# Two turned rows sent from ACT's queue at an output burst, bursts of 6, 6 and 4 column blocks, and some roundings given to ACT

## The chip, the core and the metric

The kernel runs on one core of a Trainium2 chip. The core has five engines that work side by side, each through its own list of instructions in order: TensorE (PE in the profile; its weight loads are PEld), VectorE (DVE), ScalarE (ACT), GpSimd (POOL) and SyncE (SP). A transfer between the main memory and the core's buffers is issued by one of these lists too, and an instruction that waits holds all that stand behind it in its list. The metric is the time of one execution in microseconds (us), as the median of several runs.

## The reference

Two independent results are put side by side: a multi-query attention with 32 heads that share one key and one value head, and a discrete Fourier transform over both axes of a second input.

```python
# A: x (2048 x 1024), 32 heads of 32, one head for k and v
q = (x @ wq).reshape(B, S, H, Dh).transpose(0, 2, 1, 3)
k = x @ wk
v = x @ wv
p = softmax(einsum("bhqd,bkd->bhqk", q, k) * Dh ** -0.5)
a = einsum("bhqk,bkd->bhqd", p, v).transpose(0, 2, 1, 3).reshape(B, S, H * Dh) @ wo
# B: x (2048 x 1024), DFT matrices as inputs
re = einsum("bsd,ed->bse", x, dft_hid_re)
im = einsum("bsd,ed->bse", x, dft_hid_im)
b = einsum("ts,bse->bte", dft_seq_re, re) - einsum("ts,bse->bte", dft_seq_im, im)
return concatenate([a, b], axis=-1)      # all float32
```

## The kernel before

**Two kinds of work on TensorE.** The attention's scores and exponents are one kind. All other products (q, k, v, both stages of the DFT, the product with `wo`) are the other: they are called *fill products* and are put between the attention's matmuls, so that TensorE has work while the exponents are made.

**Fill products.** Each float32 operand is split into a rounded part (`hi`) and the difference that is left (`lo`), and a product of two blocks is three matmuls (hi·hi, hi·lo, lo·hi). A `Group` is one result of 128 x 512 with its left and right blocks. A block (`Item`) goes through four stages, which class `Line` counts in `n[0]` to `n[3]`: 0 `load` (from SP's queue), 1 `comb` (a sum or difference with a second source, on POOL), 2 `hi` (the rounding, function `cast`: on ACT in the start-up, on POOL later) and 3 `lo` (the difference, on POOL). `RL` is the line of the right blocks (tiles `r0`, `r1` as loaded, `rh`, `rl` as split), `ML` that of the left ones (`m0`, `m1`, `mh`, `ml`). The lines keep a few buffers each: `may` says whether a stage of the next block may be written yet, and `pump` writes a stage when the block's due time, counted in fill products (`pos["fill"]`), is near: 40 products ahead for the loads of right blocks and 14 for their rounding, 52 and 27 for left ones. Results go back to the main memory through `store`, nine products later, on SP's queue.

**The attention** runs in 32 units (4 query blocks of 512 x 8 groups of four heads), each of 32 steps. The loop `for n in range(total)` (line 753) writes one step: `score_step(n + 44)` makes row scores for a later unit (two matmuls into `pss`, the row maximum on DVE, and, one step later, the row exponents with their sum on ACT). `expo(n)` makes the exponents that are used: two matmuls into `pst` with the scores turned round (keys along partitions), and an exponent on ACT into a tile `p`. `pst` has one buffer and `pss` two. `level(n)` then writes some fill products, about five, so that they are spread evenly.

**The turned rows.** For each query of the unit the exponent needs two rows, the maximum and the logarithm of the sum, along the other axis. `lse_1`, `lse_1b` and `lse_2` work them out from the row maxima and sums, `lse_3` turns them on TensorE (a matmul with `ident`) and lets DVE copy the result into `mt`, and `lse_4` moves two rows of it into rows 96 and 97 of the unit's query tile `qst`, and a third (the inverse sums) to the main memory, `r_d`. A unit's first `expo` needs the two rows. In `score_step` the table `LSE` gives the step of the scores' count `e` (12 ahead of the exponents' count `r`) at which each of these is written; `TURN` is that of `lse_3`.

**The output burst.** `pv(u, k)` multiplies finished exponents with `v`. `CUT` says which of the 16 column blocks of `p` belong to each of the three bursts of a unit, and `ENDS`, twice that, at which steps they are written. A burst has four matmuls of the program per column block (eight records in the trace), all in one accumulator from `bank`, in which fill groups, bursts and `lse_3` take turns. In a step with a burst no fill products are written.

Of the kernel before, what the change touches and what calls it, by code (L numbers as in the profile page):

```python
# [16 lines left out]
P = 128  # L17
# [7 lines left out]
NC = 16  # L25
# [62 lines left out]
def tile_kernel(ctx: ExitStack, tc, xT, wq, wkv, wo, xbT, wT, cT, out):  # L88
    nc = tc.nc
    te = Ordered(tc, nc.tensor)  # L90
    act = Ordered(tc, nc.scalar)
    dve = Ordered(tc, nc.vector)
    gp = Ordered(tc, nc.gpsimd)
    sp = Ordered(tc, nc.sync)
# [11 lines left out]
    r_d = [dram.tile([NC, P], F32, name=f"r_{u}") for u in range(NQ * NG)]  # L106
# [26 lines left out]
    def move(q, to, of):  # L133
        q.dma_start(to.bitcast(F32), of.bitcast(F32))


    class Line:
# [24 lines left out]
        def pump(self):  # L162
            for k in range(4):
                while self.may(k) and self.items[self.n[k]].due - self.lead[k] <= pos["fill"]:
                    self.step(k)
# [3 lines left out]
                k = next(k for k in (3, 2, 1, 0) if self.may(k))  # L169
                self.step(k)  # L170

    pos = {"fill": 0, "s": 0}

    def cast(to, of):
        if pos["fill"] < START:
            act.activation(to, of, AF.Copy)
        else:
            gp.tensor_copy(to, of)
# [19 lines left out]
            sp.dma_start(it.t[-1], a)  # L198

    def comb(it):  # L200
        if it.pre:
            return
        for t, (_, sg) in zip(it.t[1:], it.srcs[1:]):
            (gp.tensor_add if sg > 0 else gp.tensor_sub)(it.t[0], it.t[0], t)
        if it.raw is not None:
            store(it.raw[0], it.t[0], it.raw[1])
# [39 lines left out]
    RL = Line(NR0, NR, (40, 40, 14, 8), load_r, comb, hi_r, lo)  # L246
    ML = Line(NM0, NM, (52, 36, 27, 21), load_m, comb, hi_m, lo)
# [28 lines left out]

    prev = {"set": -200, "this": 0}
    end = [0]

    def pump():  # L280
        RL.pump()
# [8 lines left out]
    def at(p, f):  # L290
        k = len(later)
        while k and later[k - 1][0] > p:
            k -= 1
        later.insert(k, (p, f))

    def run_later():
        while later and later[0][0] <= pos["fill"]:
            later.pop(0)[1]()
# [8 lines left out]
    def store(to, of, key=None):  # L307
        def go():
            move(sp, to, of)
            if key:  # L310
                ready.add(key)
        soon(go)
# [4 lines left out]
    def bank(name, open_=False):  # L317

        b = 1 - cur["bank"] if cur["bank"] is not None else int(used[1] < used[0])
        cur["at"] += 1  # L320
        used[b] = cur["at"]
        if open_:
            cur["bank"] = b
        return ps_b[b].tile([P, W], F32, name=name)
# [10 lines left out]
    def product(g, ps, j):  # L335
        c, w = divmod(j, 3)
        l, r = g.left[c // 4], g.right[c]
        a = (l.lo if w == 2 else l.hi)[:, c % 4]
        te.matmul(ps[:g.rows], a, r.lo if w == 1 else r.hi, start=j == 0, stop=j == g.n - 1)

    def take(n):
        for _ in range(n):
            if cur["group"] >= len(groups):
                return
            g = groups[cur["group"]]
            j = pos["fill"] - g.at
            if j == 0:
                cur["ps"] = bank("psb", True)
            if j % 3 == 0:
                RL.force(g.right[j // 3])  # L350
            if j % 12 == 0:
                ML.force(g.left[j // 12])
            product(g, cur["ps"], j)
            pos["fill"] += 1
            if j == g.n - 1:
                cur["group"] += 1
                assert all(hasattr(it, "done") for it in g.ys)
                g.post(cur["ps"])
                cur["at"] += 1
                used[cur["bank"]] = cur["at"]  # L360
                cur["bank"] = None
                if g.ys:
                    at(pos["fill"] + 2 * BEHIND, lambda n=len(g.ys): yused.__setitem__(0, yused[0] + n))
            pump()
            run_later()

    def aside():

        if cur["group"] >= len(groups):
            return  # L370
        g = groups[cur["group"]]
        j = pos["fill"] - g.at
        if 0 < j < 6:
            take(6 - j)
        elif j > g.n - 6:
            take(g.n - j)
# [180 lines left out]
    START = 24 * len(start)  # L557
# [13 lines left out]
    units = [(b, g) for b in range(NQ) for g in range(NG)]  # L571
    SU = 32
    LEAD = 12
    total = SU * len(units)
    qst, nm, lse, pt, ov, rb, pend = ({} for _ in range(7))
    ends = []

    def open_unit(u):
        b, g = units[u]
        assert ("q", b, g) in ready  # L580
        if u < 3:
            rows.append(qsp.tile([P, 4, W], F32R, name=f"qst{u}"))
            gp.memset(rows[u][96:P].bitcast(F32), 0.0)
        q = rows[u % 3]
        if u >= 3:
            move(sp, q[96:98].rearrange("p a b -> p (a b)"), kst[98:100])
        for r, src in enumerate((qh_d, ql_d, qh_d)):
            move(sp, q[r * DH:(r + 1) * DH], src[b][g].rearrange("(h d) c -> d h c", d=DH))
        qst[u] = q
        nm[u] = sm.tile([P, 10, NC], F32, name="nm")  # L590
# [43 lines left out]
    def lse_3(u):  # L634
        aside()
        pm = bank("psb")
        te.transpose(pm[:3 * NC, :P], nm[u][:, 3:6].rearrange("p a b -> p (a b)"), ident)
        mt = sm.tile([3 * NC, P], F32, name="mt")
        dve.tensor_copy(mt, pm[:3 * NC, :P])
        cur["at"] += 1  # L640
        lse[u] = mt

    def lse_4(u):
        mt = lse.pop(u)
        for a in range(2):
            move(sp, qst[u][96 + a:97 + a].rearrange("o h (t c) -> o (h t) c", c=P), mt[a * NC:(a + 1) * NC])
        sp.dma_start(r_d[u], mt[2 * NC:])

    def inverse(u):
        rb[u] = onp.tile([P, W], F32, name="rb")  # L650
# [10 lines left out]
            te.matmul(ps[:, a], kst[:, c * P:(c + 1) * P], qst[u][:, 2 * hp_ + a], start=True, stop=True)  # L661
        act.activation(pt[u, c, hp_], ps, AF.Exp)

    CUT = (0, 6, 11, NC)

    def pv(u, k):

        aside()
        ps = bank("psb")
        for c in range(CUT[k], CUT[k + 1]):  # L670
            for h in range(4):
                te.matmul(ps[h * DH:(h + 1) * DH], v[:, c], pt[u, c, h // 2][:, h % 2], start=c == CUT[k], stop=c == CUT[k + 1] - 1)
        if k == 0:
            ov[u] = onp.tile([P, W], F32, name="ov")
            dve.tensor_copy(ov[u], ps)
        else:
            dve.tensor_add(ov[u], ov[u], ps)
        cur["at"] += 1
        if k == len(CUT) - 2:
            b, g = units[u]  # L680
            hi_ = onp.tile([P, W], F32R, name="oh")
            lo_ = onp.tile([P, W], F32R, name="ol")
            lse["out"] = hi_, lo_

            last = u + 1 == len(units)
            e = dve if last else gp

            def low():
                e.tensor_sub(lo_, ov[u], hi_.bitcast(F32))
                if not last:  # L690
                    store(oh_d[b][g], hi_)
                    store(ol_d[b][g], lo_, ("o", b, g))

            ends.append(lambda: e.tensor_mul(ov[u], ov[u], rb[u]))
            ends.append(lambda: e.tensor_copy(hi_, ov[u]))
            ends.append(low)

    def score_step(s):

        if s < total:  # L700
            u, r = divmod(s, SU)
            if r == SU - 6 and u + 1 < len(units):
                open_unit(u + 1)
        if SU <= s < SU * (len(units) + 1) and s % SU == TURN:
            lse_3((s - SU) // SU)
        if s < total:
            scores(s)
        row_sums(s - 1)
        u, e = divmod(s - SU, SU)
        if 0 <= u < len(units):  # L710
            for f in LSE.get(e, ()):
                f(u)

    TURN = 6
    LSE = {1: (lse_1,), 2: (lse_1b,), 4: (lse_2,), 8: (lse_4,)}

    room = [(lambda t=t, k=k: t[:, k]) for t in [pp.tile([P, 2, W], F32, name="p") for _ in range(NP)] for k in range(2)]
    for n, (it, to) in enumerate(zip(RL.items, room)):
# [7 lines left out]
    take(66)  # L726
    for s in range(SU + LEAD):
        score_step(s)
        take(7)

    PRO = pos["fill"]
# [7 lines left out]
    def goal(n):  # L739
        return PRO + (FILL - PRO - LAST - MORE * (total - QUIET)) * n // total + MORE * max(n - QUIET, 0)  # L740


    ENDS = [2 * c for c in CUT]

    def level(n):
        r = n % SU
        if r in ENDS:
            return
        more = min(e for e in ENDS if e > r) - r
        left = goal(n + more) - pos["fill"]  # L750
        take(left - left * (more - 1) // more)

    for n in range(total):
        u, r = divmod(n, SU)
        if n == total - 12:
            w1 = wo_set(1)
            add([o_group(NQ - 1, t, e, ws) for e, ws in ((0, w0), (1, w1)) for t in range(4)])
        score_step(n + SU + LEAD)
        if ends:
            ends.pop(0)()  # L760
        expo(n)
        if r == 16:
            inverse(u)
        if r in ENDS and n:
            pv((n - 1) // SU, (ENDS.index(r) - 1) % (len(CUT) - 1))
        level(n)


    last = groups[len(groups) - 8:]
    take(last[0].at - pos["fill"] - 12)  # L770
    pv(len(units) - 1, len(CUT) - 2)
    while ends:
# [66 lines left out]
```

## Time and profile before

| | |
|---|---|
| median of 3 runs | 2813.01 us (2805.11 to 2813.58) |
| the profiled execution | 2811.13 us, span 2809.3 us |
| mean granted clock of TensorE | 0.996 |
| busy: TensorE, ACT, DVE, POOL | 2767.0, 2176.8, 1601.6, 1598.2 us |
| transfers | 489.73 MB, 174 GB/s in the mean |

All instructions carry line 66, that of the helper `Ordered` that records them, so groups are told apart by their tiles: `psb<-rh,mh` is a fill product, `pss<-kst,qst` row scores, `pst<-qst,kst` the turned scores, `psb<-p,v` a burst. In the table of waits a row names who waited, for whom, the total in us, how often and the longest. In the order of time a row has the start, the length, the engine and the instruction, and in brackets how long the engine idled before it and for whom. In a table of stretches a row has the stretch, its length, busy time and number of instructions of each engine, the granted clock, the share of the transfer engines and GB/s. SPq is SP's queue; a row there is the issue of a transfer, not its landing. The chain's rows have a start, a length and what the chain spent it on; a transfer there lasts from issue to landing.

### The profile page before, as it was taken

The numbers are of one execution on the slowest core, as the hardware profiler recorded it, in microseconds if no ns is written. First come the engines' busy times: TensorE is split into PE (matmuls) and PEld (weight loads), VectorE is DVE, ScalarE is ACT, GpSimd is POOL, SyncE is SP. The second block draws the span as 40 slices with busy tenths as digits, with TensorE's granted clock in tenths as the row PEclk, the third lists the DMA queues.
The fourth block names the chain that finished last, engine by engine and source line by source line (L and its number), as shares of the span: only waits on it lengthen the run. The fifth ranks groups of instructions, "written<-read, shape, count | busy, mean of one in ns | idle before, by whom it ended". The sixth has DMA issues, their size and how long they took to land.

```text
span 2809.3 us, 40359 instructions
## 1 busy us (share of the span) xinstructions
PE 2767.0 (98%) x13904; PEld 1936.5 (69%) x13904; DVE 1601.6 (57%) x1832; ACT 2176.8 (77%) x3151; POOL 1598.2 (57%) x1593
## 2 busy tenths in 40 slices
PE   8999999999999999999999999999999999999999
PEld 5876676676766766767666676667666667767666
DVE  6766666666666665555555555555555556556401
ACT  4578787888878888888878888878888778888740
POOL 3754524565536447766675575797787775540110
PEclk9999999999999999999999999999999999999999
DMA  7643325675676555665554464665565553554455
GB/s 257 196 147 113 125 87 188 218 240 181 214 241 207 165 161 186 185 184 149 167 193 133 150 188 140 195 211 173 186 201 169 177 185 105 169 175 150 123 168 170
DMA packets 320449, 489.73 MB, mean 174 GB/s; under 512 B 33978, under 2 KB 99002, under 8 KB 320186
## 3 DMA queue, kind: packets, MB, share of 16 engines
q1 hardware_dynamic: 320244, 487.15, 55.2%
q8 instruction: 110, 1.80, 0.3%
q14 instruction: 95, 0.78, 0.1%
HBM read 366.22 MB, written 119.28 MB: 173 GB/s over the span
## 4 chain that ended last, share of the span: by engine, by line
PE 89%; DMA 5%; POOL 2%; issue 2%; SPq 1%; ACT 1%; DVE 1%; POOLq 0%; ACTq 0%; DVEq 0%
PE psb L66 56%; PE pss L66 17%; PE pst L66 16%; DMA r<-s 2%; SPq L66 1%; POOL ml L66 1%; DMA qst<-mt 1%; POOL mh L66 0%; DMA p<-in_xT_dram 0%; ACT pss L66 0%; DMA m<-in_cT_dram 0%; POOL rh L66 0%; DMA r<-in_xT_dram 0%; ACT p L66 0%; DMA ql<-ql 0%
## 5 line engine op out<-in xcount | busy, mean ns | idle before, releaser
L66 DVE TENSOR_REDUCE nm<-pss 128x1 f32<-128x1024 f32 x1024 | 1252.6, 1223 | 594.6 <-PE pss L66 594.0
L66 ACT ACTIVATE p<-pst 128x1024 f32<-128x1024 f32 x1024 | 1053.4, 1029 | 487.2 <-PE pst L66 485.6
L66 ACT ACTIVATE pss<-pss,nm 128x1024 f32<-128x1024 f32 x1024 | 1112.9, 1087 | 69.0 <-DVE nm L66 66.7
L66 PE MATMUL psb<-rh,mh 128*128 128x512 f32 (+1 forms) x1852 | 730.9, 395 | 14.0 <-ACT rh L66 8.1
L66 PE MATMUL psb<-rh,ml 128*128 128x512 f32 (+1 forms) x1852 | 730.8, 395 | 6.4 <-POOL ml L66 6.4
L66 PE MATMUL psb<-rl,mh 128*128 128x512 f32 (+1 forms) x1852 | 729.2, 394 | 0.3 <-DVE rl L66 0.3
L66 PE MATMUL pst<-qst,kst 128*128 128x512 f32 x2048 | 654.4, 400 | 11.8 <-DMA qst<-mt 11.2
L66 PE MATMUL pss<-kst,qst 128*128 128x512 f32 x2048 | 654.8, 400 | 2.0 <-ACT pss L66 1.6
L66 PEld LDWEIGHTS pss<-kst,qst 128*128 128x128 f32 x2048 | 375.2, 188 | 162.8 <-issue 76.5
L66 POOL TENSOR_TENSOR ml<-m,mh 128x512 fp32r<-128x512 f32 x340 | 439.6, 1293 | 49.9 <-ACT mh L66 40.1
L66 PEld LDWEIGHTS pst<-qst,kst 128*128 128x128 f32 x2048 | 374.7, 188 | 128.8 <-ACT p L66 32.7
L66 PE MATMUL psb<-p,v 128*32 128x512 f32 x4096 | 462.5, 598 | 0.0
L66 PEld LDWEIGHTS psb<-rh,mh 128*128 128x128 f32 (+1 forms) x1852 | 346.9, 187 | 101.7 <-ACT rh L66 9.4
L66 PEld LDWEIGHTS psb<-rh,ml 128*128 128x128 f32 (+1 forms) x1852 | 346.8, 187 | 91.7 <-POOL ml L66 8.5
L66 PEld LDWEIGHTS psb<-rl,mh 128*128 128x128 f32 (+1 forms) x1852 | 346.8, 187 | 84.4 <-DVE rl L66 1.4
L66 POOL TENSOR_TENSOR r<-r,r 128x512 f32<-128x512 f32 x120 | 154.7, 1290 | 315.3 <-DMA r<-s 172.1
L66 PEld LDWEIGHTS psb<-p,v 128*32 128x32 f32 x4096 | 123.7, 110 | 286.9 <-issue 279.4
L66 POOL CAST mh<-m 128x512 fp32r<-128x512 f32 x339 | 208.3, 615 | 172.3 <-PE psb L66 155.9
L66 POOL CAST rh<-r 128x512 fp32r<-128x512 f32 x214 | 131.9, 616 | 264.2 <-PE psb L66 139.4
L66 POOL TENSOR_TENSOR rl<-r,rh 128x512 fp32r<-128x512 f32 x214 | 276.6, 1293 | 3.9
L66 POOL TENSOR_TENSOR m<-m,m 128x512 f32<-128x512 f32 x200 | 258.5, 1293 | 31.7 <-DMA m<-in_xbT_dram 19.6
L66 ACT ACTIVATION_READ_ACCUMULATOR pss<-pss,nm 128x1 f32 x1024 | 210.5, 206 | 0.0
(62 smaller groups left out, 690.5 us busy)
## 6 DMA issues: line engine op xcount, KB each, us to landing
m<-in_cT_dram SPq DMA_DIRECT2D x384, 256.0 KB
r<-s SPq DMA_DIRECT2D x192, 256.0 KB
y<-y SPq DMA_DIRECT2D x128, 256.0 KB
r<-in_wT_dram SPq DMA_DIRECT2D x88, 256.0 KB
m<-in_xbT_dram SPq DMA_DIRECT2D x88, 256.0 KB
y<-u SPq DMA_DIRECT2D x80, 256.0 KB
m<-in_wq_dram SPq DMA_DIRECT2D x64, 256.0 KB
qst<-qh SPq DMA_DIRECT2D x64, 256.0 KB
```

The costliest lines, as they stand in the source:

```text
L66: return lambda *a, **k: self.tc.keep_in_program_order(f(*a, **k))
```

## The change

Four things are changed.

1. `lse_4` issues its three transfers from ACT's queue instead of SP's. It is no longer called from `LSE` but from the main loop, behind the burst, in the step with `(r + LEAD) % SU == TURN`, which is r = 24.
2. `TURN` goes from 6 to 4, and `LSE` from steps 1, 2, 4 (and 8 for `lse_4`) to 0, 1, 2.
3. `CUT` goes from 0, 6, 11, 16 to 0, 6, 12, 16: the bursts have 6, 6 and 4 column blocks and stand behind steps 12, 24 and 32 (32 is step 0 of the next unit) instead of 12, 22 and 32.
4. `ahead(6)`, called at the end of each burst, writes up to six roundings of blocks whose `comb` was written at least 12 fill products ago, the nearest due first, and `cast` gives these to ACT. In the built program that is never more than one in a burst: 42 roundings, all of right blocks.

```diff
-    pos = {"fill": 0, "s": 0}
+    pos = {"fill": 0, "s": 0, "act": False}
 
     def cast(to, of):
-        if pos["fill"] < START:
+        if pos["fill"] < START or pos["act"]:
             act.activation(to, of, AF.Copy)
...
     def comb(it):
+        it.at = pos["fill"]
...
+    def ahead(n):
+        pos["act"] = True
+        for _ in range(n):
+            lines = [x for x in (RL, ML) if x.may(2) and not x.items[x.n[2]].pre and pos["fill"] - x.items[x.n[2]].at >= 12]
+            if not lines:
+                break
+            min(lines, key=lambda x: x.items[x.n[2]].due).step(2)
+        pos["act"] = False
...
     def lse_4(u):
         mt = lse.pop(u)
         for a in range(2):
-            move(sp, qst[u][96 + a:97 + a].rearrange("o h (t c) -> o (h t) c", c=P), mt[a * NC:(a + 1) * NC])
-        sp.dma_start(r_d[u], mt[2 * NC:])
+            move(act, qst[u][96 + a:97 + a].rearrange("o h (t c) -> o (h t) c", c=P), mt[a * NC:(a + 1) * NC])
+        act.dma_start(r_d[u], mt[2 * NC:])
...
-    CUT = (0, 6, 11, NC)
+    CUT = (0, 6,12, NC)
...
             dve.tensor_add(ov[u], ov[u], ps)
+        ahead(6)
         cur["at"] += 1
...
-    TURN = 6
-    LSE = {1: (lse_1,), 2: (lse_1b,), 4: (lse_2,), 8: (lse_4,)}
+    TURN = 4
+    LSE = {0: (lse_1,), 1: (lse_1b,), 2: (lse_2,)}
...
         score_step(s)
+        if s == SU + TURN:
+            lse_4(0)
         take(7)
...
             pv((n - 1) // SU, (ENDS.index(r) - 1) % (len(CUT) - 1))
+        if (r + LEAD) % SU == TURN and u + 1 < len(units):
+            lse_4(u + 1)
         level(n)
```

The order on ACT, around step 24 of the unit before unit 16 (units are counted from 0; `p` is an exponent that is used, `pss` row exponents; in brackets the semaphores that are waited for, DMAHW0 to DMAHW7 being those of transfers). Before, ACT has exponents alone there:

```order
L66 ACTIVATE p_13846<-pst_13847 128x1024 [waits PE_49]
L66 ACTIVATE pss_13841,nm_13607<-pss_13841,nm_13607 128x1024 [waits DVE_49,Activation_49]
L66 ACTIVATE p_13872<-pst_13873 128x1024 [waits PE_49]
L66 ACTIVATE pss_13859,nm_13607<-pss_13859,nm_13607 128x1024 [waits DVE_49,Activation_49]
L66 ACTIVATE p_13906<-pst_13907 128x1024 [waits PE_49]
L66 ACTIVATE pss_13901,nm_13607<-pss_13901,nm_13607 128x1024 [waits DVE_49,Activation_49]
L66 ACTIVATE p_13927<-pst_13928 128x1024 [waits PE_49]
```

In the changed kernel, between step 24's exponent and the next row exponents:

```order
L66 ACTIVATE pss_13830,nm_13609<-pss_13830,nm_13609 128x1024 [waits DVE_49,Activation_49]
L66 ACTIVATE p_13854<-pst_13855 128x1024 [waits PE_49]
L66 ACTIVATE rh_13885<-r0_13735 128x512 [waits Pool_49]
L66 DMA qst1_1499<-mt_13847 1x16x128 [waits DMAHW1_49,DVE_49]
L66 DMA qst1_1499<-mt_13847 1x16x128 [waits DMAHW6_49]
L66 DMA r_16_145<-mt_13847 16x128 [waits DMAHW3_49]
L66 ACTIVATE pss_13849,nm_13609<-pss_13849,nm_13609 128x1024 [waits DVE_49,Activation_49]
L66 ACTIVATE p_13896<-pst_13897 128x1024 [waits PE_49]
L66 ACTIVATE pss_13891,nm_13609<-pss_13891,nm_13609 128x1024 [waits DVE_49,Activation_49]
```

A rounding and the three transfers of unit 16's rows now stand ahead of the row exponents; each transfer waits for a semaphore of another transfer.

The order on SP at the same place of the program. Before, the three transfers stand among the loads:

```order
L66 DMA y_1_1_4_269<-y0_13703 128x512 [waits DMAHW0_49]
L66 DMA m0_13935<-in_cT_dram 128x512 [waits DMAHW1_49,Pool_49]
L66 DMA y0_13957<-hs_1_6_393 128x512 [waits DMAHW2_49]
L66 DMA y0_13959<-y_1_1_6_271 128x512 [waits DMAHW3_49]
L66 DMA qst1_1499<-mt_13920 1x16x128 [waits DMAHW4_49,DVE_49]
L66 DMA qst1_1499<-mt_13920 1x16x128 [waits DMAHW5_49]
L66 DMA r_16_145<-mt_13920 16x128 [waits DMAHW6_49]
L66 DMA r0_13984<-s01_7_338 128x512 [waits DMAHW7_49]
```

In the changed kernel:

```order
L66 DMA m0_13791<-in_cT_dram 128x512 [waits DMAHW7_49,Pool_49]
L66 DMA m1_13793<-in_cT_dram 128x512 [waits DMAHW0_49]
L66 DMA y0_13823<-hs_1_5_392 128x512 [waits DMAHW2_49]
L66 DMA y0_13825<-y_1_1_5_270 128x512 [waits DMAHW3_49]
L66 DMA r0_13903<-s01_6_337 128x512 [waits DMAHW4_49,Activation_49]
L66 DMA r1_13905<-s11_6_369 128x512 [waits DMAHW5_49]
L66 DMA m0_13908<-in_cT_dram 128x512 [waits DMAHW7_49,Pool_49]
L66 DMA m1_13910<-in_cT_dram 128x512 [waits DMAHW0_49]
```

The transfers of `mt` are gone from SP. The semaphores are dealt to the transfers of both queues in turn, so SP's rows skip those that ACT's took (here 1, 6 and, two rows on, 3): ACT's third transfer, which waits for DMAHW3, waits for the load `y0_13825<-y_1_1_5_270`.

The order on TensorE. Before, the second burst of that unit, of 20 matmuls, stands at step 22:

```order
L66 MATMUL pss<-kst,qst_2184 128x512 x2
L66 MATMUL pst<-qst_868,kst 128x512 x2
L66 MATMUL psb<-rh,ml 128x512
L66 MATMUL psb<-p,v 32x512 x20
L66 MATMUL pss<-kst,qst_2184 128x512 x2
L66 MATMUL pst<-qst_868,kst 128x512 x2
L66 MATMUL psb<-rh,mh 128x512
```

and the turning matmul (`ident`) at step 26, among fill products:

```order
L66 MATMUL psb<-rh,ml 128x512
L66 MATMUL psb<-rh,mh 128x512
L66 MATMUL psb<-rl,mh 128x512
L66 MATMUL psb<-ident,nm 48x128
L66 MATMUL pss<-kst,qst_2184 128x512 x2
L66 MATMUL pst<-qst_868,kst 128x512 x2
```

In the changed kernel both are in step 24:

```order
L66 MATMUL psb<-rh,mh 128x512
L66 MATMUL psb<-rl,mh 128x512
L66 MATMUL psb<-rh,ml 128x512
L66 MATMUL psb<-ident,nm 48x128
L66 MATMUL pss<-kst,qst_2170 128x512 x2
L66 MATMUL pst<-qst_868,kst 128x512 x2
L66 MATMUL psb<-p,v 32x512 x24
L66 MATMUL pss<-kst,qst_2170 128x512 x2
L66 MATMUL pst<-qst_868,kst 128x512 x2
```

The turning matmul and the burst of 24 now follow each other with four matmuls between them.

## Prediction

> **What bounds the kernel now.** I read the page's busy times and chain first, then the table of waits, SP's own with it.
>
> ```profile
> PE 2767.0 (98%) x13904; PEld 1936.5 (69%) x13904; DVE 1601.6 (57%) x1832; ACT 2176.8 (77%) x3151; POOL 1598.2 (57%) x1593
> PE 89%; DMA 5%; POOL 2%; issue 2%; SPq 1%; ACT 1%; DVE 1%; POOLq 0%; ACTq 0%; DVEq 0%
> ...
> PE pst L66 <- DMA qst<-mt: 11.2, 5, 4.4
> PE psb L66 <- POOL ml L66: 6.4, 4, 2.3
> PE psb L66 <- POOL mh L66: 3.5, 2, 1.9
> ...
> SPq L66 <- POOL ml L66: 899.5, 245, 14.9
> SPq L66 <- DVE mt L66: 25.7, 17, 6.4
> ```
>
> TensorE sets the time: the change does not alter its number of matmuls, so it can only add or take waits of TensorE. The largest of these that the change touches is the wait of the first exponent matmul of a unit for the two turned rows (11.2 us, 5 times), then the waits for POOL's roundings and differences (9.9 us). SP's row is the one to keep in mind: its queue stands for a third of the span behind POOL's `ml`, because a load of the next left block needs the buffer that `ml` frees.
>
> Next the order of time in an ordinary step and in a burst.
>
> ```profile
> 1000.50 1.09 ACT L66 ACTIVATE pss<-pss,nm 128x1024 f32<-128x1024 f32 x1
> 1000.70 0.63 PE L66 MATMUL pss<-kst,qst 128*128 128x512 f32 x2
> 1001.51 0.19 ACT L66 ACTIVATION_READ_ACCUMULATOR pss<-pss,nm 128x1 f32 x1
> 1001.83 1.03 ACT L66 ACTIVATE p<-pst 128x1024 f32<-128x1024 f32 x1
> 1002.79 0.63 PE L66 MATMUL pss<-kst,qst 128*128 128x512 f32 x2
> ...
> 1014.24 4.50 PE L66 MATMUL psb<-p,v 128*32 128x512 f32 x40
> 1016.35 0.19 ACT L66 ACTIVATION_READ_ACCUMULATOR pss<-pss,nm 128x1 f32 x1
> 1019.90 1.03 ACT L66 ACTIVATE p<-pst 128x1024 f32<-128x1024 f32 x1 [3.36 <-PE pst L66]
> ```
>
> A step takes 2.09 us of TensorE (1000.70 to 1002.79) and just as much of ACT: outside a burst ACT has nothing to spare. Inside a burst of five column blocks ACT idles 3.36 us; with six blocks it is 0.9 us more (4.50/5), with four as much less.
>
> The third view is the clock around the three longest waits for turned rows that follow each other in the trace.
>
> ```profile
> 1443.70:1446.30 2.60, 0.59 (x3) 0.41 (x3) 1.23 (x1) 0.71 (x2) 1.88 (x2) 1.00 0.81 265
> 1446.30:1449.70 3.40, 3.40 (x19) 0.78 (x21) 0.69 (x1) 2.12 (x3) 2.52 (x3) 0.50 0.70 231
> 1855.30:1859.80 4.50, 0.15 (x1) 0.00 (x0) 1.23 (x1) 0.69 (x2) 3.53 (x3) 0.94 0.87 311
> 1859.80:1866.10 6.30, 6.25 (x25) 2.48 (x29) 0.69 (x1) 2.12 (x3) 5.32 (x6) 0.50 0.57 172
> 2273.90:2276.70 2.80, 0.36 (x3) 0.11 (x2) 1.23 (x1) 1.04 (x2) 1.33 (x2) 1.00 0.61 214
> 2276.70:2280.10 3.40, 3.40 (x26) 1.61 (x30) 0.69 (x1) 2.12 (x3) 2.38 (x3) 1.00 0.47 150
> ```
>
> Of three waits over 2 us, two (1443.7 and 1855.3) are followed by a stretch at a granted clock of 0.50, of 3.4 and 6.3 us; the third (2273.9) is not. Such a stretch costs half its length.
>
> **The change, part by part.**
>
> *Turned rows.* They are now issued right after the burst that follows step 24 instead of in step 28, and need not stand in SP's queue. All five waits should go: −11.2 us, and with them the two half-clock stretches, −(3.4 + 6.3)/2 = −4.9 us. The least I can grant is −11.2 us, the most −16.1 us. The Trainium skill (TensorE: Matmul & The Clock Gate, "Why this matters for your kernels") asks for idle gaps over about 3 us before the clock falls; by it only the 1855 wait would bring a stretch, and this gain would be 14.4 us. The trace shows the stretch at 1446.3 behind a shorter one, so here the measurement decides.
>
> *Issuing on ACT.* The cost of an issue is known from SP, the cost of a rounding from the first group.
>
> ```profile
> L66 SPq DMA_DIRECT2D qst<-mt x64: 503/571/1104, 147.8 to 2664.8; - x64
> L66 SPq DMA_DIRECT2D r<-mt x32: 567/569/768, 149.2 to 2665.4; - x32
> L66 ACT ACTIVATE rh<-r 128x512 fp32r<-128x512 f32 x8 | 5.1, 632 | 7.2 <-DMA r<-in_xT_dram 7.1
> L66 POOL CAST rh<-r 128x512 fp32r<-128x512 f32 x214 | 131.9, 616 | 264.2 <-PE psb L66 139.4
> ```
>
> Three issues (2 × 0.57 + 0.57 = 1.7 us) and at most one rounding (0.63 us) per burst make 2.3 us, under the 4.2 us of a six-block burst; a burst of four has 2.5 us for its one rounding. By themselves they cost 0. If ACT's cover were gone they would cost 32 × 1.7 + 42 × 0.63 = 81 us, the far end.
>
> *The wait that comes with them.* The program gives its transfers eight completion semaphores in turn, and each waits until the transfer eight places before it has landed. On SP's queue that wait held up loads. On ACT it stands ahead of the exponents of the next step. So ACT now waits for transfers of SP, which wait for POOL. Where POOL's work closes a ring with its loads, SP is late:
>
> ```profile
> 1416.52 5.52 DMA r<-s
> 1423.38 0.61 POOL mh L66
> 1424.00 0.56 POOL rh L66
> 1425.77 1.31 POOL ml L66
> 1429.38 5.65 DMA r<-s
> 1442.05 3.69 DMA qst<-mt
> ...
> 1103.07 0.81 SPq L66 DMA_DIRECT2D m<-in_cT_dram  x2
> 1427.10 0.81 SPq L66 DMA_DIRECT2D m<-in_cT_dram  x2
> 1427.81 0.39 PE L66 MATMUL pss<-kst,qst 128*128 128x512 f32 x1
> 1428.42 0.43 SPq L66 DMA_DIRECT2D y<-y  x1
> 1926.99 0.80 SPq L66 DMA_DIRECT2D m<-in_cT_dram  x2
> 2007.31 0.43 SPq L66 DMA_DIRECT2D y<-hs  x1
> 2258.55 0.90 SPq L66 DMA_DIRECT2D r<-s  x2
> 2259.07 0.63 PE L66 MATMUL pss<-kst,qst 128*128 128x512 f32 x2
> ```
>
> The first six rows are the chain through such a ring (load, POOL, SP, load, some 13 us a turn); the others are SP's issues in units 12, 16, 22, 23 and 26, with the first matmul after step 24 in units 16 and 26. For each of the 32 units I looked up which transfer stands eight places before the third one on ACT, and when it was issued, counted from that matmul. In six units (12, 16, 21, 22, 23, 26) it comes at −0.3, +0.6, −1.0, −0.5, −0.4 and −0.5 us, together −2.1. The burst ends 0.9 us later in the changed kernel, so −7.5 for six. Landing takes 3.7 to 5.6 us by the chain's rows; with 4.6 the six land 27.6 − 7.5 = 20.1 us past the burst's end in sum. Then ACT issues the third transfer (0.6) and works off the row exponents (1.09 + 0.19), against one step of TensorE's (2.1 us) before it needs their buffer: 0.2 us under; and with one exponent still between it and the next it gets some 0.4 us more. So each unit costs what the landing is late plus 0.2: 21 us. With 3.7 and 5.6 us it is 16 and 27 us. Three more units (11, 18, 28) had the transfer late only because a product group ended just there; the group now ends before the burst, and I put 0 to 3 us each, 3 in all. Sum +24 us, between 0 (if SP, freed of its 25.7 us behind `mt`, is never late) and 36.
>
> *Its half clock.* Waits of units 16, 23 and 26 would be some 4 us, and 28's up to 3. By two in three that left a stretch of 3.4 us, three stretches: +5 us; 0 to 10.
>
> *Roundings.* 42 of POOL's 616 ns roundings go, 26 us of its 1598; off the chain they are worth nothing. In the ring a rounding is one link of 0.56 us. Four of the moved ones stand in turns that ended in a wait of TensorE for `ml`: −2.2 us; from 0 to the whole 9.9. A rounding that waited on POOL's sum would hold ACT; the rule of 12 products (some 6 us) leaves time.
>
> *Bursts 6, 6, 4.* The same matmuls. The 13 buffers already carry a first burst of six. Transposing now shares its step, and so its accumulator, with the burst, which must wait for DVE's copy; four matmuls (0.9 us) stand between. +1 us, up to 10 if DVE is in another sum each time. The row maxima's earlier steps cost 0: DVE is busy for 57%.
>
> *Sum.* 2811.1 (span 2809.3 and 1.8 around it) − 11.2 − 4.9 − 2.2 + 24 + 5 + 1 = 2822.8 us, against the profiled execution. The median of the runs is 1.9 us above it, and I leave the sum at 2823, 0.35% over that median. A measurement of this kernel tells about 0.3% from no change, 8.4 us.
>
> **The rivals.**
>
> *Faster: ACT is hardly held.* For it speaks that in 23 of 32 units the transfer eight places before had landed by the burst's end, and that six blocks give all queues 5.4 us to catch up. If what SP does is driven by TensorE's products rather than by POOL's ring, each landing moves 4 to 5 us ahead, and the 24 and 5 us vanish: 2811.1 − 18.3 + 1 = 2794; from 2787 with more of POOL's waits gone, to 2804. Against it: in the rows above POOL works without a gap but for its load. It decides where the six landings come under 0.5 us past the burst. The Trainium skill (DMA: Bandwidth & Descriptors, "Issuing engines are not separate DMA queues") says that transfers of all engines run on the same 16 DMA engines, and that another issuer only saves sequencer time; by it the new queue itself gives nothing and the earlier step gives all, which is this rival's time. No row of this trace shows an issue on ACT.
>
> *No change: the holds are half of it.* With landings of 3.7 us and no half clock the new waits are 16 us against 18 of the old: 2811.1 − 18.3 + 16 + 1 = 2810; with landings of 4.6 us and the three units, 2818.
>
> *Much slower: the ring spreads.* If ACT's hold makes TensorE drop its clock in every one of nine units (two stretches each, 3.4 us) and landings take 5.6 us, it is 2811 − 18 + 36 + 31 = 2860.
>
> *The roundings don't come early.* Then POOL's waits stay: +2 us, within any of these.
>
> **How the numbers follow.** The forecast (new waits outweigh the old, 2816 to 2842) 0.53, of which 0.08 lie within 0.3%; the faster rival 0.27; the even one 0.13; the worst 0.07. Faster 0.27, same 0.21, slower 0.52. The range leaves out the worst and the outer parts of the faster: 2794 to 2842; the forecast's own is 2816 to 2842.
>
> **What the profile would show.** Right: no row of TensorE waiting for `qst<-mt`; ACT's queue waiting for loads, `pss` or `pst` of TensorE waiting for ACT some 20 us more in total, with single waits of 2 to 5 us one step after the burst that follows step 24, in units 12 to 28; half-clock stretches behind some. Wrong: TensorE's waits for ACT as before, then the faster rival holds; or waits in all units, which would speak for issue cost. What would upset it most is SP's lateness: if it shifts by 2 us in each unit, the forecast shifts by 12.

## The result and the profile after

| | before | after |
|---|---|---|
| median | 2810.17 us (2805.11 to 2813.58, 4 runs) | 2828.89 us (2827.11 to 2831.99, 4 runs) |
| ratio to before | | 1.0069, 95% interval 1.0048 to 1.0091 |
| the profiled execution, span | 2811.1, 2809.3 us | 2827.1, 2825.3 us |
| mean granted clock | 0.996 | 0.994 |

The changed kernel is 0.7% slower, where +0.35% was forecast (2823 us). The profiled executions stand 16.0 us apart in span. First the page of the changed kernel, its busy times, its chain, and a transfer queue that it has beside SP's (packets, MB, share of time):

```profile
PE 2770.0 (98%) x13904; PEld 1943.8 (69%) x13904; DVE 1601.4 (57%) x1832; ACT 2199.8 (78%) x3193; POOL 1575.7 (56%) x1551
...
q10 hardware_dynamic: 3072, 0.79, 0.1%
...
PE 83%; DMA 6%; POOL 4%; issue 3%; ACT 2%; DVE 1%; SPq 1%; ACTq 0%; POOLq 0%; DVEq 0%
```

TensorE has the same 13904 matmuls. ACT has 42 instructions more and POOL 42 fewer: the roundings. The chain ran 89% over TensorE before, and now 83%; POOL has two points more, DMA and ACT one each. The queue q10 is the new one of ACT, with 0.79 MB in all.

The waits of the changed kernel, of TensorE the rows that the text uses, and the new ones of ACT:

```profile
ACT pss L66 <- DMA qst<-mt: 37.2, 11, 10.7
PE pss L66 <- ACT pss L66: 26.2, 10, 6.6
ACT pss L66 <- DMA y<-y: 15.4, 4, 9.2
ACT pss L66 <- DMA m<-in_cT_dram: 15.0, 2, 8.9
...
ACT pss L66 <- DMA y<-hs: 8.7, 1, 8.7
...
PE psb L66 <- POOL ml L66: 6.4, 6, 1.7
...
PE psb L66 <- POOL mh L66: 1.6, 1, 1.6
```

TensorE's row for `qst<-mt`, 11.2 us before, is gone. In its place TensorE waits 26.2 us for ACT's row exponents (`pss`), and ACT itself waits in front of those exponents for transfers: loads of SP's (`y<-y`, `m<-in_cT_dram`, `y<-hs`) and, by name, its own `qst<-mt`. That name can mislead: the longest wait of that row, 10.7 us in unit 26, ended when a load of SP's had landed and ACT could issue its third transfer, as the chain below shows.

Each wait of TensorE behind step 24, in the order of time (start of the matmul that waited, and in brackets how long), for units 12, 16, 21, 22, 23, 26 and 28:

```profile
1104.99 0.74 PE L66 MATMUL pss<-kst,qst 128*128 128x512 f32 x2 [0.58 <-ACT pss L66]
1433.75 1.22 PE L66 MATMUL pss<-kst,qst 128*128 128x512 f32 x2 [5.12 <-ACT pss L66]
1845.63 0.73 PE L66 MATMUL pss<-kst,qst 128*128 128x512 f32 x2 [0.77 <-ACT pss L66]
1932.67 0.74 PE L66 MATMUL pss<-kst,qst 128*128 128x512 f32 x2 [3.47 <-ACT pss L66]
2018.62 0.73 PE L66 MATMUL pss<-kst,qst 128*128 128x512 f32 x2 [3.70 <-ACT pss L66]
2271.83 1.22 PE L66 MATMUL pss<-kst,qst 128*128 128x512 f32 x2 [6.62 <-ACT pss L66]
2437.79 0.73 PE L66 MATMUL pss<-kst,qst 128*128 128x512 f32 x2 [3.77 <-ACT pss L66]
```

They make 24.0 us. How one of them comes about is seen in the chain through unit 26 (start, length, what):

```profile
2261.30 1.29 POOL ml L66
2262.61 0.33 SPq L66
...
2264.45 5.67 DMA r<-s
2270.15 0.32 ACTq L66
2270.57 0.10 ACT pss L66
...
2271.83 1.22 PE pss L66 x2
```

The burst had its 48 matmuls from 2257.34 on for 5.36 us. In that time POOL still worked on a left block. Only when `ml` was done (2262.6) did SP get past its load of the next left block and issue the loads behind it; one of them, `r<-s`, landed at 2270.1, 5.67 us later. In the built program that load stands eight transfers ahead of ACT's third transfer, so ACT could issue this one only then, and the row exponents behind it followed. The second transfer had been held as well: the first went out at 2259.16, the second 8.4 us later, as another load from the same place of SP's list (`m<-in_cT_dram`, issued at 2262.98) landed. ACT's list shows the second issue and the wait as a whole:

```profile
2267.58 0.51 ACTq L66 DMA_DIRECT2D qst<-mt  x1
...
2270.57 1.09 ACT L66 ACTIVATE pss<-pss,nm 128x1024 f32<-128x1024 f32 x1 [10.74 <-DMA qst<-mt]
```

The clock around the five waits of 3.4 us and more:

```profile
1432.30:1439.10 6.80, 5.35 (x13) 3.97 (x14) 1.23 (x1) 5.34 (x8) 5.60 (x6) 0.50 0.50 172
1934.10:1937.50 3.40, 3.40 (x9) 2.62 (x9) 1.27 (x2) 2.54 (x5) 3.02 (x4) 0.50 0.35 120
2019.40:2022.80 3.40, 3.26 (x8) 2.59 (x9) 1.21 (x1) 3.18 (x6) 3.40 (x4) 0.50 0.24 90
2268.60:2275.40 6.80, 3.57 (x8) 2.67 (x9) 1.23 (x1) 4.61 (x7) 4.47 (x5) 0.50 0.47 169
2439.20:2442.70 3.50, 3.50 (x11) 2.67 (x10) 0.58 (x1) 2.56 (x5) 0.61 (x1) 0.51 0.21 80
```

Each of the five has a stretch at half clock, 23.9 us in all. Two began while TensorE still waited (1.45 and 3.23 us of them), so 19.2 us passed at work, and half of that, 9.6 us, is lost.

The balance of the two spans, in us: waits for turned rows −11.2, the half clock behind them −4.9; waits for POOL from 9.9 to 8.0, −1.9; waits for `pss` from 1.6 to 26.2, +24.6; half clock behind those, +9.6. That is +16.2, beside 16.0 measured. TensorE's remaining rows of waits differ by +0.9 us together, so the fit is closer than the working deserves. The other half-clock stretches, behind POOL's waits and in the start-up, are 10.2 us long in both kernels.

### The profile page after: what moved, and what is told of

It is laid out like the page before. It is cut to its first block, busy times and chain, and to the rows that moved or that the text cites. A ratio compares the mean times of both kernels' runs of the same rounds, so it can differ in the third digit from the quotient of the medians.

```text
span 2825.3 us, 40461 instructions
## 1 busy us (share of the span) xinstructions
PE 2770.0 (98%) x13904; PEld 1943.8 (69%) x13904; DVE 1601.4 (57%) x1832; ACT 2199.8 (78%) x3193; POOL 1575.7 (56%) x1551
## 4 chain that ended last, share of the span: by engine, by line
PE 83%; DMA 6%; POOL 4%; issue 3%; ACT 2%; DVE 1%; SPq 1%; ACTq 0%; POOLq 0%; DVEq 0%
PE psb L66 52%; PE pss L66 16%; PE pst L66 15%; DMA r<-s 3%; POOL ml L66 1%; ACT pss L66 1%; SPq L66 1%; DMA m<-in_cT_dram 1%; ACT p L66 1%; DVE nm L66 1%; POOL mh L66 1%; POOL m L66 0%; DMA p<-in_xT_dram 0%; POOL rh L66 0%; POOL y L66 0%
## 5 line engine op out<-in xcount | busy, mean ns | idle before, releaser
L66 PE MATMUL psb<-rh,mh 128*128 128x512 f32 (+1 forms) x1852 | 732.7, 396 | 10.2 <-ACT rh L66 8.6
L66 PE MATMUL pss<-kst,qst 128*128 128x512 f32 x2048 | 657.5, 402 | 26.7 <-ACT pss L66 26.2
L66 POOL CAST rh<-r 128x512 fp32r<-128x512 f32 x172 | 106.2, 618 | 225.3 <-PE psb L66 134.3
```

The lines of the kernel that those rows point to most:

```text
L66: return lambda *a, **k: self.tc.keep_in_program_order(f(*a, **k))
```

## The experiments

The theory was the prediction's: on ACT's queue each of the three transfers waits until the transfer eight places ahead, mostly one of SP's, has landed, and this holds the exponents behind it. The main rival was that the loss comes from the work the change puts on ACT or into the burst (issues, roundings, longer bursts), the second that it comes from a second queue as such. Ratios are to the kernel before, run beside each group of experiments.

| kernel | median, us | ratio, 95% interval |
|---|---|---|
| the change | 2828.89 | 1.0069 (1.0048 to 1.0091) |
| transfers back on SP, same step | 2793.59 | 0.9950 (0.9934 to 0.9967) |
| the change without roundings | 2824.97 | 1.0062 (1.0047 to 1.0077) |
| before, with roundings alone | 2803.67 | 0.9988 (0.9979 to 0.9998) |
| only the third transfer on SP | 2805.72 | 0.9995 (0.9986 to 1.0005) |
| before, with the earlier step alone (SP) | 2792.11 | 0.9961 (0.9946 to 0.9976) |
| the change with bursts 6, 5, 5 | 2866.12 | 1.0223 (1.0204 to 1.0241) |
| transfers on SP, without roundings | 2794.45 | 0.9970 (0.9958 to 0.9981) |
| transfers on SP, a dummy hold on ACT | 2960.87 | 1.0562 (1.0545 to 1.0580) |
| transfers on POOL's queue | 2792.99 | 0.9947 (0.9930 to 0.9963) |
| transfers on SP, bursts 6, 5, 5 | 2791.72 | 0.9941 (0.9926 to 0.9956) |

**The queue alone.** The changed kernel, with the transfers issued by SP at the same place of the program:

```diff
-            move(act, qst[u][96 + a:97 + a]...
-        act.dma_start(r_d[u], mt[2 * NC:])
+            move(sp, qst[u][96 + a:97 + a]...
+        sp.dma_start(r_d[u], mt[2 * NC:])
```

> The changed kernel, with its three transfers of the turned rows issued from SP's queue again, at the same place of the program (behind the burst after step 24). Theory (the queue: on ACT the transfers wait for landings of SP's transfers and hold the exponents behind them): TensorE's wait for the row exponents falls from 26.2 us to under 3 us, the half-clock stretches behind it go, the old wait for the turned rows (11.2 us) does not come back, because the rows are still issued four steps earlier: 2796 us, 2790 to 2803, faster than the kernel before. Rival (the work: the larger second burst, the turning matmul beside it, the roundings on ACT): the time stays at 2822 to 2832 us.

Measured: 2793.59 us. TensorE's waits there:

```profile
PE psb L66 <- POOL ml L66: 9.7, 7, 1.7
PE psb L66 <- POOL mh L66: 2.5, 2, 1.6
PE pss L66 <- ACT pss L66: 1.8, 2, 1.3
```

Neither the waits for turned rows nor those for ACT are left. ACT's busy time is 2200.0 us, as in the changed kernel. So the step, the bursts and the roundings together gain 0.5%, and the queue turns this into a loss of 0.7%. The spans differ by 31.6 us: 24.4 in `pss` waits, some 10 in half clock, while the waits for POOL are 4.2 us shorter on ACT's queue (a TensorE that is held gives POOL time, which was not tried by itself).

**The roundings, out of the change and alone.** In the first kernel the call `ahead(6)` is taken out of `pv`; in the second it is the only thing added to the kernel before.

```diff
-        ahead(6)
```

> The changed kernel without the 42 roundings on ACT at the bursts; POOL does them as before. Theory (the queue): the holds of ACT stay in units 12, 16, 21, 22, 23, 26 and 28, some 25 us in all, and POOL gets 26 us of work back, worth 0 to 4 us on the chain: 2829 to 2834 us. Rival (the roundings hold ACT, since they wait for POOL's sums): the time falls by 10 us or more, to under 2819 us.

> The kernel before with the roundings at its bursts alone (bursts of 6, 5 and 5, transfers on SP in step 28). Theory: ACT has 2.5 us or more to spare in a burst for one rounding of 0.63 us, and POOL's ring gets 0.56 us shorter in a few turns: 2806 to 2812 us, that is 0 to 4 us faster than before. Rival (the roundings cost, because ACT waits for POOL's sum in them): 2815 us or more.

Measured: 1.0062 without them, and 0.9988 with them alone. The holds stay without the roundings:

```profile
PE pss L66 <- ACT pss L66: 20.6, 8, 5.0
```

Of the 20.6 us, 19.5 stand in units 16, 21, 22, 23, 26 and 28; the time came out some 4 us under the expectation. Alone they shorten the waits for POOL's `ml`:

```profile
PE pst L66 <- DMA qst<-mt: 10.7, 5, 4.2
PE psb L66 <- POOL ml L66: 3.1, 2, 1.7
```

3.1 us in place of 6.4, and about as much of the time (0.12%, 3.4 us). Inside the change their worth is not resolved: the intervals with and without them overlap, though the waits for POOL are 12.4 us without them and 8.0 us with them.

**One transfer of the three on SP.** If ACT waits for a certain transfer eight places ahead, taking the third transfer off ACT must change which units are held.

```diff
-        act.dma_start(r_d[u], mt[2 * NC:])
+        sp.dma_start(r_d[u], mt[2 * NC:])
```

> The changed kernel with only the third transfer, the inverse sums to the main memory, on SP's queue; the two turned rows stay on ACT. The transfer eight places ahead of the last one on ACT is then another: in units 16, 21 and 23 one that landed 0.4 to 4.6 us before step 24's end in the trace of the kernel before, in unit 26 still a late one (landed 3.6 us after it), in units 12, 18, 22 and 28 the third transfer itself, which SP can issue as soon as it has got there. Theory (the eighth transfer back): the holds go in 16, 21 and 23, one of some 3 us stays in 26; if SP gets to the third transfer in time in 12, 22 and 28, TensorE's wait for the row exponents is 2 to 8 us in all and the time 2797 to 2808 us. Rival (any transfer on ACT costs about the same): two thirds of the loss stay, 2815 to 2824 us.

Measured: 2805.72 us, a ratio of 0.9995. The long waits behind step 24 are now these three:

```profile
2084.57 0.74 PE L66 MATMUL pss<-kst,qst 128*128 128x512 f32 x2 [1.30 <-ACT pss L66]
2253.64 1.22 PE L66 MATMUL pss<-kst,qst 128*128 128x512 f32 x2 [6.21 <-ACT pss L66]
2417.35 0.73 PE L66 MATMUL pss<-kst,qst 128*128 128x512 f32 x2 [0.67 <-ACT pss L66]
```

Units 16, 22 and 23, each held by 3.5 to 5.1 us in the changed kernel, are free; unit 24, free there, is held; unit 26 is held for 6.21 us, which the expectation had put too low. In units 24 and 26 it is the second transfer, now ACT's last, that was held: it went out 7.1 and 9.4 us after the first, each time as a load of SP's (`m<-in_cT_dram`, `y<-hs`) landed. Two issues of three still stand on ACT in every unit, so the issue itself does not explain the holds.

**The earlier step alone.** The kernel before with `TURN`, `LSE` and the place of the call from the change, on SP's queue, with the old bursts and no roundings:

```diff
-    TURN = 6
-    LSE = {1: (lse_1,), 2: (lse_1b,), 4: (lse_2,), 8: (lse_4,)}
+    TURN = 4
+    LSE = {0: (lse_1,), 1: (lse_1b,), 2: (lse_2,)}
...
+        if (r + LEAD) % SU == TURN and u + 1 < len(units):
+            lse_4(u + 1)
```

> Only the earlier step of the turned rows, on SP's queue: bursts as before, no roundings on ACT. Theory (the earlier step alone ends the waits for the turned rows and the half-clock stretches behind them): no wait of TensorE for qst<-mt, and 2793 to 2799 us beside 2808 before, since -11.2 and -4.9 us are owed to that part and the roundings alone gave 3 us. Rival (the rows come in time only because they leave right behind a burst of six, or because POOL was relieved): some of the waits for qst<-mt stay and the time is 2802 us or more.

Measured: 2792.11 us, just under the expected band; 0.9961, with no wait for `qst<-mt`. So the whole gain for the turned rows belongs to the step, not to the queue or the burst. The two kernels that keep the step on SP's queue and differ in the rest stand beside it. Without roundings, with the new bursts:

> The transfers on SP's queue at step 24 with bursts 6, 6 and 4, without the roundings on ACT. If the roundings are worth some 3 us whatever the queue, as they were alone: 2796 to 2799 us beside 2793.6 with them, and TensorE's waits for POOL's ml and mh 3 to 8 us in place of 12. If they only moved POOL's waits, 2791 to 2795 us, no difference.

It gave 0.9970, against 0.9950 with the roundings: of the size of what they gave alone, but the intervals overlap. The bands in us did not decide, since the kernel before ran some 6 us lower in this group, and the waits for POOL came to 16.0 us, up from 12.2, not to 3 to 8.

And with roundings, with the old bursts:

> The transfers on SP's queue at step 24 with the roundings on ACT, but bursts of 6, 5 and 5 as before, so that no burst follows step 24. On SP's queue nothing of TensorE's or ACT's stands behind the transfers, so the place of the burst should not matter as it does on ACT's queue (where the same exchange cost 37 us): ratio to before 0.994 to 0.998, as for the kernel with bursts of 6, 6 and 4 (0.995). If the burst's place matters by itself: over 1.000.

It gave 0.9941: on SP's queue the burst's place does not matter.

**The burst's cover taken away.** The changed kernel, transfers on ACT, with the bursts of before, so that none stands beside step 24:

```diff
-    CUT = (0, 6,12, NC)
+    CUT = (0, 6, 11, NC)
```

> The changed kernel with bursts of 6, 5 and 5 column blocks as before, so that ACT issues the three transfers two steps behind a burst, with no burst beside the issue. Theory (the issues, 1.7 us a unit, are hidden only by the burst; ACT has nothing to spare in an ordinary step): short waits of TensorE for ACT in most of the 31 units, 0.5 to 1.7 us each, beside the long ones of units 12, 16, 21, 22, 23, 26 and 28, and 2840 to 2890 us. Rival (the issue costs nothing anyway, only the late transfers do): waits in the same few units as in the changed kernel, 2825 to 2835 us.

Measured: 2866.12 us, in the theory's band, but not by the waits that it named. Here are TensorE's waits for ACT, and two single ones, of units 16 and 24:

```profile
PE pss L66 <- ACT pss L66: 55.6, 11, 11.2
...
PE pst L66 <- ACT p L66: 3.0, 15, 0.4
...
1446.80 1.22 PE L66 MATMUL pss<-kst,qst 128*128 128x512 f32 x2 [8.50 <-ACT pss L66]
2126.63 1.22 PE L66 MATMUL pss<-kst,qst 128*128 128x512 f32 x2 [11.15 <-ACT pss L66]
```

No short waits in most of the units: eight single ones make 54.4 of the 55.6 us, in units 12, 16, 21, 22, 23, 24, 26 and 28. The issues on ACT cost TensorE nothing even in ordinary steps, within 0.5 us a unit: ACT issues while its exponent before them still runs, and stands still for only some 1.0 us, as here in unit 15:

```profile
1354.75 1.09 ACT L66 ACTIVATE pss<-pss,nm 128x1024 f32<-128x1024 f32 x1 [1.01 <-DMA qst<-mt]
```

What the burst covers is the late transfer: in the six units that are held in both kernels, and longer here (12, 16, 21, 23, 26, 28), the wait is 2.3 to 4.8 us longer, 3.6 in the mean, somewhat under the 4.2 us that ACT idles in a burst of six. The 3.6 us are not shown to be the cover's alone, for the semaphores fall on other transfers here in part: unit 24, free in the changed kernel, is held for 11.15 us by its second and third transfers, and unit 22 for less than there (0.91 us). The mean granted clock falls to 0.990.

**A hold of known size.** The transfers are on SP's queue, and ACT makes 26 copies that nothing uses where its issues stood:

```diff
+            for _ in range(26):
+                act.activation(idle, ident, AF.Copy)
```

> A hold of known size: the transfers stay on SP's queue at step 24, and at that place ACT makes 26 copies of a 128x128 tile that nothing uses (estimate 0.31 us each from its rows of 128x32 and 128x512, 8.0 us in all, against 4.2 us of idle time in the burst) in each of the 31 units. TensorE should be held some 3.5 to 4.5 us in each, about 125 us in all. Theory (a hold of this size costs more than itself, since a stretch of 3.4 or 6.8 us at half clock follows most of them, as behind five of seven in the changed kernel): 31 times 1 to 1.5 us more, 2950 to 2970 us, mean clock under 0.985. Rival (the stretches of the changed kernel belong to its late loads, not to the hold): 2905 to 2930 us and a clock of 0.993 or more.

Measured: 2960.87 us, with a clock of 0.977. The copies as a group, TensorE's waits, and the stretches around the hold of unit 1 (one in the wait, then the one with its end and what follows):

```profile
L66 ACT ACTIVATE idle<-ident 128x128 f32<-128x128 f32 x806 | 249.7, 310 | 24.6
...
PE pss L66 <- ACT pss L66: 107.9, 32, 4.5
...
218.00:221.00 3.00, 0.00 (x0) 0.00 (x0) 0.00 (x0) 2.78 (x9) 0.33 (x1) 1.00 0.29 87
221.00:227.80 6.80, 6.07 (x14) 4.60 (x15) 1.71 (x2) 4.80 (x8) 0.00 (x0) 0.50 0.00 0
```

The holds are 3.1 to 4.5 us each, 107.9 us of waits rather than the expected 125. Of 31 holds 30 have a stretch at half clock behind them, of 3.4 us or of 6.8. The clock of 0.977 over 2955.7 us is a loss of 68 us, against 6 in the same kernel without the copies (0.998 of 2793.7): 62 us for 31 holds, 2.0 us each, above the 1 to 1.5 us expected; a little of it passed while TensorE still waited. No late load is part of these holds, so the half clock belongs to the hold.

**Another queue without the shared semaphores.** The transfers are issued by POOL. In the built program they wait for `mt` alone:

```diff
-            move(act, qst[u][96 + a:97 + a]...
-        act.dma_start(r_d[u], mt[2 * NC:])
+            move(gp, qst[u][96 + a:97 + a]...
+        gp.dma_start(r_d[u], mt[2 * NC:])
```

> The changed kernel with the three transfers on POOL's queue, at the same place. In the built program POOL's transfers take no turn of the eight semaphores that SP's and ACT's share, so none of them waits for a load; each stands ahead of POOL's next rounding. Theory (the loss comes from the shared semaphores and from what is queued behind them on ACT): no wait of TensorE for ACT's pss over 1.5 us, no half clock behind such waits, and 2790 to 2806 us beside 2805 before; up to 10 us of it in longer waits for POOL's ml and mh, since three issues (0.57 us each on SP) stand in POOL's ring with its loads. Rival (any second queue beside SP's brings the loss, for the transfers then run against the loads): waits of the size of the changed kernel, 2820 us or more.

Measured: 2792.99 us. POOL's issues, and TensorE's waits:

```profile
L66 POOL DMA_DIRECT2D qst<-mt x64 | 33.0, 517 | 111.5 <-DVE mt L66 111.5
...
PE psb L66 <- POOL ml L66: 8.0, 7, 1.7
PE pss L66 <- ACT pss L66: 2.6, 2, 2.0
```

A queue beside SP's does not bring the loss. POOL idles 111.5 us until DVE has written `mt`, and TensorE does not feel it: its waits for `ml` are 8.0 us, under the 9.7 us with SP's queue.

The three best (2791.7 to 2793.6 us, ratios 0.9941 to 0.9950) have the step and the roundings of the change with the transfers on SP's or POOL's queue, and beat both kernels; the runs don't tell them from each other.

## Why the prediction was right, and where a size was off

- *Turned rows, −11.2 and −4.9.* Right: the row is gone, and alone the earlier step gained 0.39% (0.24 to 0.54%, 7 to 15 us), somewhat under the 16.1 us of the two terms; TensorE's waits for POOL were 1.5 us longer there (11.4 us). That the queue itself gives nothing also held: SP's and POOL's do as well.
- *Issuing on ACT, 0.* Right, but the cover was misnamed. The prediction hid the 1.7 us in the burst and put 81 us on their far end without it; with the burst gone, the units without a late transfer show no wait. "Outside a burst ACT has nothing to spare" was the step that failed there: ACT made up a pause of about 1.0 us before TensorE felt it.
- *The wait that comes with them, +24.* Right in place; that the size fits too is in part luck. The six units named first are held for 20.3 us (21 forecast), and of the three doubtful ones unit 28 is held for 3.77 us, 11 and 18 not at all (3 forecast in all). But two steps behind the 21 were off, against each other. First, counted from the first matmul behind the burst, ACT's third transfer went out 1.5, 6.0, 1.7, 4.4, 4.6 and 7.5 us late in units 12, 16, 21, 22, 23 and 26. That makes 25.7 us in all, not 20.1: SP issued the six loads 7.7 us later in sum than the prediction put them, and their landings took 4.2 us in the mean rather than 4.6. Second, each unit cost 0.9 us less than its transfer was late, not 0.2 us more. TensorE's first and last matmul between burst and wait in unit 26 show why:

```profile
2262.62 0.72 PE L66 MATMUL pss<-kst,qst 128*128 128x512 f32 x2
...
2264.80 0.40 PE L66 MATMUL psb<-rh,ml 128*128 128x512 f32 x1
```

  TensorE had 2.6 us of work there (2262.62 to 2265.20) rather than the 2.1 us of a step, and from ACT's third issue to TensorE's next matmul only 1.7 us passed (2270.15 to 2271.83). The prediction also looked at the third transfer alone, and the second can hold ACT as well. Why SP came later is not shown.
- *Its half clock, +5.* This is the term whose total was mis-sized: it measured 9.6 us. Three stretches of 3.4 us were taken, from two in three waits of the trace of before; all five waits of 3.4 us and more had one, two of them double. That is 4.6 us more, and the profiled execution (2827.1 us) lies 4.3 us above the sum (2822.8). The Trainium skill's condition (TensorE: Matmul & The Clock Gate, "Why this matters for your kernels"), idle gaps over about 3 us, fits the five here and the two it would spare, 0.58 and 0.77 us, better than the two in three I used. It is not the whole of it: the wait at 1443.7 in the kernel before, which had a stretch behind it, was of 2.01 us (its row is in the last section).
- *Roundings, −2.2.* Waits for POOL fell by 1.9 us, near the forecast, but not by the roundings alone: without them the changed kernel has 12.4 us of these waits, more than the 9.9 of the kernel before. The intervals don't resolve their part of its time.
- *Bursts, +1.* No matmul of the changed kernel waits for DVE's `mt`; only weight loads do, 6.3 us in 16 times, 0.5 us at most. On SP's queue the kernels with the old and the new bursts can't be told apart: 0 rather than 1.
- *The rivals.* "ACT is hardly held" gave 2794 us as its time, and that is what the kernels give whose transfers hold none of ACT's work. The Trainium skill's rule that I set beside it (DMA: Bandwidth & Descriptors, "Issuing engines are not separate DMA queues"), that another issuer only saves sequencer time, agrees with SP against POOL (0.9950 and 0.9947), and not with ACT (1.0069), where the wait for an earlier landing came with the issue. The "much slower" rival was wrong as to the change, though its clock part, a stretch behind every long hold, came true for five.

The median moved somewhat more (+0.69%) than the two profiled executions (+0.57%); that rest lies within the interval.

## What to carry to other kernels

Before a transfer is moved to a compute engine's queue, look in the built program at which earlier transfer its semaphore makes it wait for, and who is late in issuing that one; the price is not the issue but the work queued behind it, and only a pause that the engine has anyway at that place (4.2 us of ACT here) takes off from it. Change the step and the queue in separate kernels: here the step gained 0.4% and the queue lost 1.2%. Count some 2 us more for each TensorE wait of over 3 us, for the work that passes at half clock behind it: the loss was 1.9 us in the mean behind five such waits of the changed kernel, 2.0 us behind seven in the kernel without cover, though these lasted 4.8 to 11.2 us, and 1.9 us behind the 31 of the dummy copies; behind four in the kernel without roundings it was 2.5 us.

## What the runs showed of the hardware beyond the forecast

The half clock came in pieces of 3.4 us or whole multiples of it (3.4, 6.8, and 10.2 us at the waits of 11.15 and 8.88 us in the kernel without cover). It may begin within the wait, as 3.23 us before its end in unit 26, and what passes there costs nothing more. Behind a hold of 3.1 to 4.5 us it came 30 times in 31. Shorter waits had one as well. This row is of the kernel before, where the stretch at 1446.3 that the prediction showed follows:

```profile
1445.88 0.84 PE L66 MATMUL pst<-qst,kst 128*128 128x512 f32 x2 [2.01 <-DMA qst<-mt]
```

And in the changed kernel TensorE waited 1.58 and 1.25 us for POOL, 2.5 us apart, and the clock stood at 0.51 from the first of them on.

```profile
1824.79 0.77 PE L66 MATMUL psb<-rh,mh 128*128 128x512 f32 x1 [1.58 <-POOL mh L66]
1827.25 0.79 PE L66 MATMUL psb<-rh,ml 128*128 128x512 f32 x1 [1.25 <-POOL ml L66]
...
1824.80:1831.70 6.90, 5.65 (x13) 3.96 (x14) 1.22 (x1) 1.95 (x5) 6.90 (x7) 0.51 0.37 106
```

What sets the number of pieces stays open: holds of about the same length had one or two.
